# Transposes of the softmax blocks on the two row halves of the array

## The chip, the core and the metric

The kernel runs on one core of a Trainium2 chip. TensorE (PE) multiplies matrices and writes to PSUM, which has eight banks of 512 fp32 per partition; VectorE (DVE), ScalarE (ACT) and GpSimd (POOL) work on what lies in PSUM and SBUF, and DMA queues, issued by SyncE (SP), move data to and from HBM. The metric is the device time of one execution in microseconds.

## What is computed

Block-causal attention over 8 batches, 8 heads, 576 positions of 64 numbers, and an MLP block behind it with a layer norm:

```
scores = q @ k.T / 8, only where block_i >= block_j (blocks of 64 positions)
attn = softmax(scores);  x = attn @ v            # heads side by side: 512 columns
xn = (x - mean(x)) / sqrt(var(x) + 1e-6) * g
out = x + relu(xn @ w_ch1) @ w_ch2               # 512 -> 2048 -> 512
```

All inputs and the output are fp32.

## The kernel before

The first part of the time is attention. It goes by pairs of heads: 32 pairs, four to a batch. In a pair, each head's 64 numbers of q and k lie on one half of the 128 partitions, so the matmul of the scores uses 64 rows of the array, and the two heads use the two row halves (`mm`, L425; the planner's mode 64). The queries are taken 128 at a time: block rows i = 1 to 4, with 64 (2 i + 1) keys each. Rows 2 and 1 are the low scores (`s1`, two banks, softmax in the tile `pu`); rows 4 and 3 the high ones (`sab`, two tiles of two banks, softmax in `pab`). For each block row and head a pass on DVE (L443) copies the scores to SBUF, masks them and takes their extreme, which ends up in `nm`; ACT then makes the exponentials and their sums (L446).

For the products with v the keys must lie on the partitions, so each 128 x 128 cell of a softmax block is transposed on PE (`turn`, L455): `nc.tensor.transpose` with the cell as weights and the identity as moving operand, fp32. Four cells fill a PSUM bank (`new_tr`), which ACT or DVE copies to SBUF (`evac`, line 234 or 236 of the helper `copy`): two banks of the low blocks to `pt1`, four of the high blocks to `pt0`. Then come the products with v (`pv`, L461 and L465), each head on one column half of the array, first those that read `pt1`, then those that read `pt0`; DVE transposes the result to rows (L539), and a DMA writes them to HBM. Four of the eight banks hold the high scores, the other four are shared by low scores, transposes and products (one pool, `"tr"`). Once in eight pairs `first` does the first 64 queries of two batches; its own transposes (`across`) are no part of the change.

Beside that run the decoding of the weights (L350 to L373) and, once a batch is done, the normalisation of the first tiles of x (L678 to L774). The second part, after some 311 us, is the MLP: products with split weights (L876, L938), in which PE is busy nearly all the time.

The order on every engine is fixed when the program is built. `Plan` lists tasks with a guessed cost, a priority and the buffers that they read, write and allocate, runs them against a clock of its own, and emits them in that order; where a task may go to one of two engines (`any_of`), it takes the one that would be done first. On PE the steps of neighbouring pairs are chained by the numbers (pair, phase) given to `pe`: scores of pair k + 1 (phases 0 and 1), transposes of pair k (2 and 3), products of pair k (4.5 and 5). A task's `mode` only adds a guessed cost (`SWITCH`) when it differs from the one before on PE. At run time each engine goes through its list in order and waits on semaphores.

Of the kernel before, what the change touches and what calls it, by code (L numbers as in the profile page):

```python
# [18 lines left out]
P = 128  # L19
# [4 lines left out]
BIAS = {'PE': 0, 'SP': 0, 'DVE': 0, 'ACT': 0, 'POOL': 0}  # L24
WARM = 12
MMO = .0134
ROUNDS = 8, 8, 8, 8, 4
TILES = sum(ROUNDS)
D_0, D_1 = 12.0, .97
# [28 lines left out]
class Plan:  # L58
# [5 lines left out]
    def add(self, eng, cost=None, fn=None, r=(), w=(), prio=0.0, size=0, alloc=(), mode=128):  # L64
        k = Task(eng if isinstance(eng, dict) else {eng: (cost, fn)}, prio, size)
        k.mode = mode
        before = {}
        for x in r:
            before.update(dict.fromkeys(x.writers))
        for x in w:  # L70
            before.update(dict.fromkeys(x.readers))
        for x in r:
            x.readers.append(k)
        for x in w:
            x.writers.append(k)
        for x in before:
            x.next.append(k)
        k.left = len(before)
        k.uses = list(dict.fromkeys(x.root for x in (*r, *w, *alloc)))
        for x in k.uses:  # L80
            x.users += 1
        k.allocs = [x for x in dict.fromkeys(x.root for x in (*w, *alloc)) if x.make]
        self.tasks.append(k)
        return k
# [117 lines left out]
def attn_mlp_kernel(ctx: ExitStack, tc: tile.TileContext, qk, qk0, v, v0, w1, w2, g, out):  # L202
# [8 lines left out]
    nc = tc.nc  # L211
# [16 lines left out]
    def any_of(fn, **costs):  # L228

        return {e: (c, lambda e=e: fn(engines[e])) for e, c in costs.items()}  # L230
# [9 lines left out]
    def kind(name, shape, dtype, bufs, space=None, tag=None, most=None):  # L240

        tag = tag or name
        plan.free.setdefault(tag, bufs)
        own = (tag, "of " + name) if most else (tag,)
        if most:
            plan.free["of " + name] = most

        def make():
            return (space or sb).tile(shape, dtype, name=name, tag=tag, bufs=bufs)

        def new():
            x = Buf(own, make)
            if space is not dram and name not in ("tr", "s1", "o"):
                x.after, last[name] = [y for y in (last.get(name),) if y], x
            return x
        return new
# [17 lines left out]
    new_tr, new_s1, new_o, new_p = (kind(n, [P, 512], F32, 4, psum, "tr") for n in ("tr", "s1", "o", "p"))  # L274
# [7 lines left out]
    def small(name, shape, dtype, most):  # L282
        return kind(name, shape, dtype, 21, None, "small", most)
# [13 lines left out]
    new_t, new_tt, new_sum = small("t", [P, 512], F32, 4), small("tt", [P, 2, 2, P], F32, 4), small("sum", [P, 2, 256], F32, 2)  # L297
    xs = [kind(f"xm{p}", [P, max(ROUNDS) // 2, 2, 2, P], F32R, 1)() for p in range(7)]
    new_xw = kind("xw", [512, P], F32, 8, dram)
# [12 lines left out]
    ident = odd.tile([P, P], F32, name="ident")  # L312
# [72 lines left out]
    HALF = slice(0, 64), slice(64, 128)  # L385

    def evac(out, in_, n, **kw):
        add(any_of(lambda e: copy(e, out(), in_()), DVE=dve(n), ACT=act(n)), **kw)

    def pe(at, phase, *args, **kw):  # L390
        steps.setdefault((at, phase), []).append(add("PE", *args, **kw))
# [3 lines left out]
    def pair(k):  # L395
        b, c = k // 4, k % 4
        prio = 100 + 10 * k
        step = [0]

        def pr():  # L400
            step[0] += 1
            return prio + .05 * step[0]
# [24 lines left out]
        def cell(i, h, ck):  # L427

            at = FIRST[i] + (128 * i if ck == 0 else 128 * (i + ck) if h else 128 * (i - ck))
            return slice(at, at + P)  # L430
# [20 lines left out]
        def turn(o, slots):  # L451

            def go():
                for n, x in enumerate(slots()):
                    nc.tensor.transpose(o.t[:, n * P:(n + 1) * P], x, ident)  # L455
            return go

        def pv(o, at, z, steps):
            def go():
# [12 lines left out]
        pu = new_pu()  # L472
# [6 lines left out]
        low = [[], []]  # L479
# [5 lines left out]
        pab = big_of[k, 0] = new_pab()  # L485
# [8 lines left out]
        done = [[], []]  # L494
# [3 lines left out]
        pt0 = big_of[k, 1] = new_pt0()  # L498
        final[k] = [*done[0], *done[1]]
        got = []  # L500

        for h in range(2):
            for i in (4, 3):
                o, x = new_tr(), Buf(parent=pt0)
                if i == 4:
                    cells = [(4, h, ck) for ck in range(1, 5)]
                    need = [done[h][0]]
                else:
                    cells = [(3, h, ck) for ck in range(1, 4)] + [(3 + h, h, 0)]
                    need = [done[h][1]] + [done[x][1 - h] for x in range(2)]  # L510
                slots = lambda cells=cells: [pab.t[:, cell(*x)] for x in cells]
                pe(k + 1, 3, 4 * .112, turn(o, slots), r=list(dict.fromkeys(need)), w=[o], alloc=[pt0], prio=pr())
                evac(lambda h=h, i=i: pt0.t[:, h, :, i - 3], lambda o=o: o.t.rearrange("p (c n) -> p c n", c=4), 512,
                     r=[o], w=[x], prio=pr())
                got.append(x)
        ob, part_o = new_o(), []
        part_o.append(Buf(parent=ob))
        pe(k + 1, 5, (4 * 256 + 128) * 4 / 2400 + .06, pv(
# [2 lines left out]

        pt1 = new_pt1()
        got = []
        for h in range(2):
            o, x = new_tr(), Buf(parent=pt1)

            cells = (1, h, 1), (2, h, 1), (1 + h, h, 0), (2, h, 2)
            slots = lambda cells=cells: [pu.t[:, cell(*x)] for x in cells]
            need = low[h] + [low[x][1 - h] for x in range(2)]
            pe(k + 1, 2, 4 * .112, turn(o, slots), r=list(dict.fromkeys(need)), w=[o], alloc=[pt1], prio=pr())  # L530
            evac(lambda h=h: pt1.t[:, h].rearrange("p c i n -> p (c i n)"), lambda o=o: o.t, 512, r=[o], w=[x], prio=pr())
            got.append(x)
        part_o.append(Buf(parent=ob))
        pe(k + 1, 4.5, (2 * 256 + 128) * 4 / 2400 + .06, pv(
            ob, 0, lambda: pt1.t[:, :, 1, 0],
# [1 line left out]
            r=[v_sb, *got], w=[part_o[1]], alloc=[ot], prio=pr(), mode=1)  # L537

        add("DVE", dve(512), lambda: nc.vector.transpose(ot.t, ob.t), r=part_o, w=[ot], prio=pr())  # L539
        rows = Buf(parent=xd[b])  # L540
# [98 lines left out]
    n = 0  # L639
# [5 lines left out]
    END = 100 + 10 * NPAIR  # L645
    FROM = [sum(ROUNDS[:n]) for n in range(len(ROUNDS))]
    GROUPS = NJ // 2
# [3 lines left out]
    def norm_tiles(n, q, prio, gate):  # L651
# [4 lines left out]
        for h in range(2):  # L656
            t = FROM[n] + ROUNDS[n] // 2 * h + q
            m, r = divmod(t, 9)
# [95 lines left out]
    def operands(n, prio):  # L754

        tts = [new_tt() for _ in range(ROUNDS[n] // 2)]
        got = {}
# [22 lines left out]
        d1, d2, use1, use2 = {}, {}, {}, {}  # L780
        Q = range(ROUNDS[n] // 2)
        for q in Q:
# [76 lines left out]
    def products(n, gp, base):  # L859
# [8 lines left out]
        def product(p, x, start, r, w, at):  # L868
# [9 lines left out]
            new = Buf(parent=x)  # L878
            add("PE", 6 * (TN / 2400 + MMO), go, r=[*held[n, m], *wr, *r], w=[new, *w], prio=base + at)
            return new  # L880
# [42 lines left out]
    def second(n, gp, hs, base):  # L923
# [3 lines left out]
        for place, s in zip(PLACES[2 * half], (*range(half, 2 * half), *range(half))):  # L927
# [12 lines left out]
            for z, cut in enumerate(cuts):  # L940
                add("PE", 6 * ((cut.stop - cut.start) / 2400 + MMO), lambda go=go, cut=cut: go(cut),
                    r=[*final[NPAIR - 1], *hs[0, h][1], *hs[1, h][1], *wr], w=[parts[z]], alloc=[yb], prio=base + place + .1 * z)
# [85 lines left out]
```

## Time and profile before

| | |
|---|---|
| device time, median of 3 runs | 1050.25 us (1049.67 to 1051.68) |
| profiled execution, span from first to last instruction | 1051.5 us |
| PE busy | 1039.6 us (99%) |
| DVE busy | 743.6 us (71%) |
| ACT busy | 525.0 us (50%) |
| POOL busy | 285.8 us (27%) |
| transposes (L455) in the chain that ended last | 7% |
| granted TensorE clock, mean | 0.996 |

Shares are means over the two parts, which have different loads, so the first part is read by itself. The clock is given in parts of 2.4 GHz; 0.50 is 1.2 GHz. An instruction's time is from its start to its modelled end, and instructions overlap, so the pace of a run of them is the distance of their starts.

### The profile page before, as it was taken

How to read it: one execution, taken by the hardware profiler on the slowest of the kernel's cores; microseconds unless marked ns; L12 is line 12 of the kernel's file. 1: busy time of each engine (PE TensorE's matmuls, PEld its weight loads, DVE VectorE, ACT ScalarE, POOL GpSimd, SP SyncE). 2: the span in 40 equal slices, each digit the busy share in tenths (PEclk: the TensorE clock that was granted, in tenths of full speed). 3: DMA queues.
4: the chain of work that ended last, by engine and by line, in shares of the span. 5: the costliest groups of instructions: out<-in, count | busy, mean ns of one | idle time of the engine just before them, and what ended most of it. 6: DMA issues, size and time to landing. Idle time of an engine off the chain costs nothing.

```text
span 1051.5 us, 18007 instructions
## 1 busy us (share of the span) xinstructions
PE 1039.6 (99%) x6264; PEld 855.0 (81%) x6264; DVE 743.6 (71%) x1631; ACT 525.0 (50%) x1264; POOL 285.8 (27%) x468
## 2 busy tenths in 40 slices
PE   9999999999999999999999999999999999999998
PEld 7887777777778888888888888888888888888997
DVE  5878999789978878885656694665685565465544
ACT  7999897889984544441433341343242322122221
POOL 0223354445433755340222240222231220000000
PEclk9999999999999999999999999999999999999999
DMA  7678889898779898758787747688657667336873
GB/s 274 205 252 265 223 282 258 226 288 291 282 255 293 299 324 240 231 215 255 225 254 208 220 179 252 186 233 261 182 190 260 217 190 248 143 111 246 299 282 123
DMA packets 238682, 248.88 MB, mean 237 GB/s; under 512 B 159488, under 2 KB 189184, under 8 KB 228352
## 3 DMA queue, kind: packets, MB, share of 16 engines
q1 hardware_dynamic: 238592, 247.74, 73.1%
q8 instruction: 49, 0.80, 0.3%
q14 instruction: 41, 0.34, 0.1%
HBM read 182.68 MB, written 65.01 MB: 236 GB/s over the span
## 4 chain that ended last, share of the span: by engine, by line
PE 90%; DVE 6%; DMA 2%; ACT 1%; issue 1%; SPq 0%; POOL 0%; DVEq 0%; ACTq 0%; POOLq 0%
PE y L938 36%; PE p L876 32%; PE tr L455 7%; PE s L425 7%; PE o L465 5%; PE o L461 3%; DVE pab L443 1%; DMA x<-xd 1%; DMA was<-wa 1%; DVE pu L443 0%; DMA xrow<-x 0%; DVE ya L950 0%; DVE x L733 0%; DVE x L678 0%; DVE sgn L359 0%
## 5 line engine op out<-in xcount | busy, mean ns | idle before, releaser
L938 PE MATMUL y<-wc,h 128*128 128x512 f32 (+1 forms) x1740 | 434.0, 388 | 0.2 <-DVE h L896 0.2
L938 PEld LDWEIGHTS y<-wc,h 128*128 128x128 f32 x1740 | 323.0, 188 | 66.1 <-DVE h L896 1.3
L950 DVE TENSOR_TENSOR ya<-y,ya 128x512 f32<-128x512 f32 x290 | 198.0, 684 | 183.6 <-PE y L938 182.1
L876 PE MATMUL p<-xm,wa 128*128 128x512 f32 (+1 forms) x960 | 221.7, 368 | 0.0
L876 PEld LDWEIGHTS p<-xm,wa 128*128 128x128 f32 x960 | 169.9, 188 | 31.5 <-issue 0.2
L876 PE MATMUL p<-xm,wb 128*128 128x512 f32 (+1 forms) x720 | 166.3, 368 | 0.0
L884 ACT COPY t<-p 128x512 f32<-128x512 f32 (+1 forms) x120 | 65.3, 544 | 168.6 <-PE p L876 166.8
L876 PEld LDWEIGHTS p<-xm,wb 128*128 128x128 f32 x720 | 127.7, 188 | 23.6
L895 ACT ACTIVATE h<-t 128x512 fp32r<-128x512 f32 (+1 forms) x120 | 62.2, 579 | 163.5 <-DVE t L889 163.2
L889 DVE TENSOR_TENSOR t<-p,t 128x512 f32<-128x512 f32 (+1 forms) x120 | 76.3, 636 | 48.1 <-PE p L876 43.3
L425 PE MATMUL s<-raw 64*128 64x224 f32 (+3 forms) x768 | 97.6, 389 | 1.7 <-DVE nm L443 1.2
L234 ACT COPY pt<-tr 128x512 f32<-128x512 f32 x166 | 87.4, 597 | 9.1 <-PE tr L455 8.0
L446 ACT ACTIVATE pab<-pab,nm 128x448 f32<-128x448 f32 (+1 forms) x128 | 91.1, 730 | 0.1
L425 PEld LDWEIGHTS s<-raw 64*128 64x128 f32 x768 | 75.3, 189 | 17.8 <-issue 5.0
L443 DVE CUSTOM_DVE_ANT_0 pab<-s,never 128x448 f32<-128x448 f32 (+1 forms) x128 | 82.7, 684 | 2.5 <-PE s L425 1.9
L465 PE MATMUL o<-pt,v 128*64 128x256 f32 (+1 forms) x768 | 80.6, 345 | 0.0
L465 PEld LDWEIGHTS o<-pt,v 128*64 128x64 f32 x768 | 55.7, 138 | 28.3 <-issue 1.1
L896 DVE SCALAR_TENSOR_TENSOR h<-t,h 128x512 fp32r<-128x512 f32 (+1 forms) x120 | 74.1, 668 | 3.9 <-ACT h L895 3.8
L353 POOL TENSOR_SCALAR mag<-mag 128x512 f32<-128x512 f32 x32 | 48.7, 1523 | 100.0 <-ACT mag L350 92.1
L690 POOL TENSOR_SCALAR norm<-norm 128x1 f32<-128x1 f32 x28 | 7.2, 258 | 248.9 <-ACT xn L687 248.9
L446 ACT ACTIVATE pu<-pu,nm 128x320 f32<-128x320 f32 (+1 forms) x128 | 64.7, 509 | 19.9 <-DVE nm L443 18.9
L455 PE MATMUL tr<-ident,pab 128*128 128x128 f32 x512 | 65.0, 279 | 5.1 <-DVE nm L443 4.2
(96 smaller groups left out, 1035.6 us busy)
## 6 DMA issues: line engine op xcount, KB each, us to landing
wc<-wcs SPq DMA_DIRECT2D x40, 1024.0 KB, 7.1
wa<-was SPq DMA_DIRECT2D x32, 1024.0 KB, 6.4
wb<-wbs SPq DMA_DIRECT2D x32, 768.0 KB, 5.5
raw<-qk SPq DMA_DIRECT2D x31, 576.0 KB, 4.9
wr<-w SPq DMA_DIRECT2D x32, 512.0 KB, 6.2
v<-v SPq DMA_DIRECT2D x32, 320.0 KB, 5.2
x<-xd SPq DMA_DIRECT2D x144, 64.0 KB, 4.0
xrow<-x SPq DMA_DIRECT2D x36, 256.0 KB, 4.2
```

What stands on the lines that cost most here:

```text
L234: e.copy(out=out, in_=in_)
L425: nc.tensor.matmul(x, raw.t[HALF[h], 0, col], raw.t[HALF[h], 1, at:at + x.shape[1]], start=True, stop=True)
L443: add("DVE", dve(n) + .01, lambda: nc.vector.tensor_tensor_reduce(out=two(p.t[:, part(i, h)]), in0=mine(), in1=two(hide), scale=-0.125, sc ...
L446: add("ACT", act(n, True) + .14, lambda: nc.scalar.activation(out=p.t[:, part(i, h)], in_=p.t[:, part(i, h)], func=AF.Exp, bias=nm.t[:, at ...
L455: nc.tensor.transpose(o.t[:, n * P:(n + 1) * P], x, ident)
L465: nc.tensor.matmul(o.t[HALF[h], at + lo:at + 256], v_sb.t[:, ck, HALF[h]], rhs(h), start=False, stop=(n == len(steps) - 1), skip_group_che ...
L876: nc.tensor.matmul(x.t[:, 0:TN], w_(l), xs[m].t[:, 0:half, o, k], start=start and k == e == 0, stop=k == 1 and e == 2, skip_group_check=True)
L884: add("ACT", act(TN), lambda: nc.scalar.copy(out=t.t[:, 0:TN], in_=x.t[:, 0:TN]), r=[r], w=[new], prio=0)
L889: add("DVE", dve(TN), lambda: nc.vector.tensor_add(t.t[:, 0:TN], x.t[:, 0:TN], t.t[:, 0:TN]), r=r, w=[new], prio=0)
L896: add("DVE", dve(TN), lambda: nc.vector.scalar_tensor_tensor(out=x.t[:, 1, 0:TN], in0=src(), scalar=0.0, in1=x.t[:, 0, 0:TN], op0=ALU.max, ...
L938: nc.tensor.matmul(yb.t[:, cut], x.t[:, l, at:at + P], wc.t[:, i, o, cut], start=i == e == 0, stop=i == 1 and e == 2, skip_group_check=end)
L950: add("DVE", dve(cut.stop - cut.start), lambda yb=yb, ya=ya, cut=cut: nc.vector.tensor_add(ya.t[:, cut], yb.t[:, cut], ya.t[:, cut]), r=[p ...
```

## The change

A task now transposes eight cells. Each cell becomes two matmuls: the upper 64 queries on the upper half of the rows, the lower 64 on the lower half, each with 64 rows and 128 columns of weights and a 64 x 64 corner of the identity; they write 64 columns each to two different banks. A bank holds eight half cells, so there are as many banks to copy as before, six a pair, but two come with each task: one task of 16 matmuls for the low blocks and one for each head's high blocks. The copy puts its 512 numbers per partition into eight runs of 64 (`turned_to`). The tasks are given mode 64, that of the scores, and the guessed cost of a cell stays at 0.112 us (`TURN`).

```diff
+TURN = .112
...
                 for n, x in enumerate(slots()):
-                    nc.tensor.transpose(o.t[:, n * P:(n + 1) * P], x, ident)
+                    for rows, to in zip(HALF, o):
+                        nc.tensor.transpose(to.t[:, 64 * n:64 * n + 64], x[rows], ident[rows, rows])
             return go
+
+        def turned_to(pt, at, o, x, to):
+            for q, src in enumerate(o):
+                x.append(Buf(parent=pt))
+                evac(lambda q=q: to()[..., 64 * q:64 * q + 64],
+                     lambda src=src: src.t.rearrange("p (c i q) -> p c i q", c=4, q=64), 512, r=[src], w=[x[-1]], prio=at)
...
-            for i in (4, 3):
-                o, x = new_tr(), Buf(parent=pt0)
...
-                pe(k + 1, 3, 4 * .112, turn(o, slots), r=list(dict.fromkeys(need)), w=[o], alloc=[pt0], prio=pr())
-                evac(lambda h=h, i=i: pt0.t[:, h, :, i - 3], lambda o=o: o.t.rearrange("p (c n) -> p c n", c=4), 512,
-                     r=[o], w=[x], prio=pr())
-                got.append(x)
+            o = [new_tr(), new_tr()]
+            cells = [x for c in range(3) for x in ((3, h, c + 1), (4, h, c + 1))] + [(3 + h, h, 0), (4, h, 4)]
+            slots = lambda cells=cells: [pab.t[:, cell(*x)] for x in cells]
+            need = [*done[h], done[1 - h][1 - h]]
+            pe(k + 1, 3, 8 * TURN, turn(o, slots), r=list(dict.fromkeys(need)), w=o, alloc=[pt0], prio=pr(), mode=64)
+            turned_to(pt0, pr(), o, got, lambda h=h: pt0.t[:, h])
...
-        for h in range(2):
-            o, x = new_tr(), Buf(parent=pt1)
...
-            pe(k + 1, 2, 4 * .112, turn(o, slots), r=list(dict.fromkeys(need)), w=[o], alloc=[pt1], prio=pr())
-            evac(lambda h=h: pt1.t[:, h].rearrange("p c i n -> p (c i n)"), lambda o=o: o.t, 512, r=[o], w=[x], prio=pr())
-            got.append(x)
+        o = [new_tr(), new_tr()]
+        cells = [x for h in range(2) for x in ((1, h, 1), (2, h, 1), (1 + h, h, 0), (2, h, 2))]
+        slots = lambda: [pu.t[:, cell(*x)] for x in cells]
+        pe(k + 1, 2, 8 * TURN, turn(o, slots), r=[*low[0], *low[1]], w=o, alloc=[pt1], prio=pr(), mode=64)
+        turned_to(pt1, pr(), o, got, lambda: pt1.t.rearrange("p h c i n -> p (h c) i n"))
```

The change moves instructions, since the planner has other tasks to place. On PE, at the third pair's scores with the transposes and products of the second pair (`pt` of a lower number is `pt1`, the other `pt0`), before:

```order
L425 MATMUL s<-raw 128x224 x4
L455 MATMUL tr<-ident,pu 128x128 x8
L455 MATMUL tr<-ident,pab 128x128 x16
L461 MATMUL o<-pt_282,v 64x256 x2
L465 MATMUL o<-pt_282,v 64x256 x2
L465 MATMUL o<-pt_282,v 64x128 x2
L461 MATMUL o<-pt_300,v 64x256 x2
```

and now:

```order
L426 MATMUL s<-raw 128x224 x4
L457 MATMUL tr<-ident,pu 128x64 x16
L457 MATMUL tr<-ident,pab 128x64 x32
L469 MATMUL o<-pt_307,v 64x256 x2
L473 MATMUL o<-pt_307,v 64x256 x2
L473 MATMUL o<-pt_307,v 64x128 x2
L469 MATMUL o<-pt_332,v 64x256 x2
```

The steps stand in the same order; each transpose has become two. This holds for all pairs but the last two, where products of the MLP (L876, now L873) now stand between the steps.

On DVE, from the first pass over the high scores to the transpose of the output, in the third pair before (in the second it is `PP00PP`, with P a pass over `pab` and 0 or 1 a copy to `pt0` or `pt1`):

```order
L443 ISA pab_290,nm_274<-s_263,never_79 128x576
...
L443 ISA pab_290,nm_274<-s_263,never_79 128x448
...
L443 ISA pab_290,nm_274<-s_264,never_79 128x576
...
L236 COPY pt0_300<-tr_313 128x4x128
L443 ISA pab_290,nm_274<-s_264,never_79 128x448
...
L539 STREAM_TRANSPOSE ot_327<-o_326 128x512
```

Now the second pair (called pair 1 below, the first being pair 0) has two copies between the passes:

```order
L444 ISA pab_200,nm_161<-s_163,never_79 128x576
...
L237 COPY pt1_181<-tr_179 128x8x64
L444 ISA pab_200,nm_161<-s_163,never_79 128x448
...
L444 ISA pab_200,nm_161<-s_164,never_79 128x576
...
L237 COPY pt0_208<-tr_230 128x8x64
L444 ISA pab_200,nm_161<-s_164,never_79 128x448
...
L536 STREAM_TRANSPOSE ot_252<-o_251 128x512
```

and the third (pair 2) has its second copy behind all four:

```order
L444 ISA pab_327,nm_298<-s_287,never_79 128x576
...
L444 ISA pab_327,nm_298<-s_287,never_79 128x448
...
L444 ISA pab_327,nm_298<-s_288,never_79 128x448
...
L237 COPY pt0_332<-tr_331 128x8x64
L444 ISA pab_327,nm_298<-s_288,never_79 128x576
...
L237 COPY pt0_332<-tr_356 128x8x64
L536 STREAM_TRANSPOSE ot_376<-o_375 128x512
```

In each of them one copy has moved from ACT to DVE. Over the whole program DVE has 61 copies out of transpose banks instead of 30, ACT 135 instead of 166.

## Rows read from the trace of the kernel before

**Rows 1.** The page: busy time of each engine; the chain that ended last.

```profile
PE 1039.6 (99%) x6264; PEld 855.0 (81%) x6264; DVE 743.6 (71%) x1631; ACT 525.0 (50%) x1264; POOL 285.8 (27%) x468
...
PE y L938 36%; PE p L876 32%; PE tr L455 7%; PE s L425 7%; PE o L465 5%; PE o L461 3%; DVE pab L443 1%; DMA x<-xd 1%; DMA was<-wa 1%; DVE pu L443 0%; DMA xrow<-x 0%; DVE ya L950 0%; DVE x L733 0%; DVE x L678 0%; DVE sgn L359 0%
```

**Rows 2.** By stretch: length, busy us of each engine, clock, DMA share, GB/s.

```profile
19.25:311.00 291.75, 286.04 (x2737) 225.79 (x2736) 250.84 (x747) 261.69 (x704) 112.13 (x140) 0.99 0.81 255
311.00:1051.50 740.50, 736.84 (x3414) 616.01 (x3413) 482.39 (x849) 250.38 (x525) 172.97 (x323) 1.00 0.70 228
```

**Rows 3.** PE in order of time, one pair: start, length, what, count.

```profile
19.25 2.86 PE L425 MATMUL s<-raw 64*128 64x320 f32 x24
22.04 1.09 PE L455 MATMUL tr<-ident,pu 128*128 128x128 f32 x8
22.97 1.91 PE L455 MATMUL tr<-ident,pab 128*128 128x128 f32 x16
24.81 0.65 PE L461 MATMUL o<-pt,v 128*64 128x256 f32 x4
...
25.94 0.60 PE L461 MATMUL o<-pt,v 128*64 128x256 f32 x4
26.37 1.68 PE L465 MATMUL o<-pt,v 128*64 128x256 f32 x16
27.98 0.54 PE L425 MATMUL s<-raw 64*128 64x320 f32 x2
```

**Rows 4.** Weight loads (PEld) in order of time: a run's first, its first two.

```profile
22.04 0.14 PEld L455 LDWEIGHTS tr<-ident,pu 128*128 128x128 f32 x1 [0.28 <-issue]
...
22.04 0.20 PEld L455 LDWEIGHTS tr<-ident,pu 128*128 128x128 f32 x2 [0.28 <-issue]
```

**Rows 5.** PE in order of time: matmuls of 64 columns on four quarters.

```profile
36.72 0.69 PE L577 MATMUL tr<-qk 64*64 64x64 f32 x32
```

**Rows 6.** DVE in order of time, the same pair; in brackets idle time before.

```profile
22.14 0.76 DVE L443 CUSTOM_DVE_ANT_0 pab<-s,never 128x576 f32<-128x576 f32 x1 [0.26 <-PE s L425]
...
23.36 0.75 DVE L443 CUSTOM_DVE_ANT_0 pab<-s,never 128x576 f32<-128x576 f32 x1
...
24.48 0.69 DVE L236 COPY pt<-tr 128x512 f32<-128x512 f32 x1 [0.35 <-PE tr L455]
25.08 0.62 DVE L443 CUSTOM_DVE_ANT_0 pab<-s,never 128x448 f32<-128x448 f32 x1
...
28.10 0.72 DVE L539 STREAM_TRANSPOSE ot<-o 128x512 f32<-128x512 f32 x1 [2.39 <-PE o L465]
```

**Rows 7.** ACT in order of time, the same pair.

```profile
22.73 2.05 ACT L234 COPY pt<-tr 128x512 f32<-128x512 f32 x4
```

**Rows 8.** Groups by line: count, busy us, mean ns, idle us before.

```profile
L455 PE MATMUL tr<-ident,pab 128*128 128x128 f32 x512 | 65.0, 279 | 5.1 <-DVE nm L443 4.2
...
L234 ACT COPY pt<-tr 128x512 f32<-128x512 f32 x166 | 87.4, 597 | 9.1 <-PE tr L455 8.0 <-issue 0.2
...
L236 DVE COPY pt<-tr 128x512 f32<-128x512 f32 x30 | 20.7, 689 | 9.1 <-PE tr L455 8.6 <-PE tr L606 0.2
```

**Rows 9.** What DVE waited for, 0 to 315 us: total, times, longest.

```profile
DVE ot L539 <- PE o L465: 24.3, 22, 2.7
DVE pt L236 <- PE tr L455: 8.6, 21, 0.8
```

**Rows 10.** By stretch, as rows 2: the densest of DVE.

```profile
131.00:158.00 27.00, 27.00 (x247) 21.51 (x245) 25.48 (x80) 24.98 (x69) 14.80 (x26) 1.00 0.85 279
```

**Rows 11.** PE's two longest waits in a transpose stage; the stretches behind them.

```profile
179.26 0.63 PE L455 MATMUL tr<-ident,pab 128*128 128x128 f32 x4 [1.72 <-DVE nm L443]
...
193.79 2.45 PE L455 MATMUL tr<-ident,pab 128*128 128x128 f32 x12 [1.64 <-DVE nm L443]
...
180.50:184.00 3.50, 3.50 (x18) 2.57 (x18) 3.43 (x14) 2.96 (x8) 2.21 (x12) 0.51 1.04 381
194.00:197.70 3.70, 3.70 (x20) 2.80 (x20) 3.47 (x13) 2.60 (x7) 0.70 (x1) 0.54 0.96 173
```

More of the change, by code (lines that the diff above doesn't have):

```diff
@@ L502, in pair @@
         for h in range(2):
-            for i in (4, 3):
-                o, x = new_tr(), Buf(parent=pt0)
[L505 to L511, printed above, removed]
-                pe(k + 1, 3, 4 * .112, turn(o, slots), r=list(dict.fromkeys(need)), w=[o], alloc=[pt0], prio=pr())
-                evac(lambda h=h, i=i: pt0.t[:, h, :, i - 3], lambda o=o: o.t.rearrange("p (c n) -> p c n", c=4), 512,
-                     r=[o], w=[x], prio=pr())
-                got.append(x)
+            o = [new_tr(), new_tr()]
[4 more added lines that the diff above has]
+            turned_to(pt0, pr(), o, got, lambda h=h: pt0.t[:, h])
         ob, part_o = new_o(), []
@@ L523, in pair @@
         got = []
-        for h in range(2):
-            o, x = new_tr(), Buf(parent=pt1)
-            cells = (1, h, 1), (2, h, 1), (1 + h, h, 0), (2, h, 2)
-            slots = lambda cells=cells: [pu.t[:, cell(*x)] for x in cells]
-            need = low[h] + [low[x][1 - h] for x in range(2)]
-            pe(k + 1, 2, 4 * .112, turn(o, slots), r=list(dict.fromkeys(need)), w=[o], alloc=[pt1], prio=pr())
-            evac(lambda h=h: pt1.t[:, h].rearrange("p c i n -> p (c i n)"), lambda o=o: o.t, 512, r=[o], w=[x], prio=pr())
-            got.append(x)
+        o = [new_tr(), new_tr()]
[3 more added lines that the diff above has]
+        turned_to(pt1, pr(), o, got, lambda: pt1.t.rearrange("p h c i n -> p (h c) i n"))
         part_o.append(Buf(parent=ob))
```

## The prediction

> **What bounds the kernel now.** I read the page's totals first, then the table by stretch, then one pair on each engine in order of time, and last who waits for whom. TensorE is busy for 99% of the span, and the transposes are 7% of the chain that ended last [rows 1]. The change touches only the attention, so the stretch to look at is 19.25 to 311 us, 31 of the 32 pairs: there PE is busy 286.0 of 291.75 us, but VectorE (DVE) 250.8 and ScalarE (ACT) 261.7 [rows 2]. So PE sets the pace, and two engines stand close behind it. After 311 us PE is busy 736.8 of 740.5 us [rows 2], with nothing in it that the change makes shorter.
>
> One pair on PE [rows 3], counted from the start of its scores at 19.25: transposes of the pair before begin at 2.79, the products with v of its low blocks (pt1) at 5.56, those of its high blocks (pt0) at 6.69, the next scores at 8.73. Nothing lies between them but short turns of the mode: PE is the loop. DVE meanwhile makes four passes over the high scores (pab), one copy out of a transpose bank, and then stands 2.39 us until the products end [rows 6].
>
> **What PE saves.** Sixteen transposes take 1.91 us, of which the last is 0.28 long [rows 3, 8]: (1.91 - 0.28) / 15 = 109 ns each. A block becomes two matmuls of 64 columns on the two row halves. The halves of the scores already run side by side, but no row shows a transpose there, so its pitch is bounded: from below by half of 109, 54 ns; from above by the 32 matmuls of 64 columns on four quarters, 0.69 us for eight rounds, 86 ns [rows 5]. Between them lies the weight load: the first load of the transposes begins at 22.04 and takes 0.14, two of them 0.20, so the second begins 0.06 behind the first [rows 4]. I take 60 ns, since each half must load 128 columns per block and this row is the load itself. The saving is 24 x (109 - 60) = 1.18 us a pair (0.55 to 1.3).
>
> The turn from scores to transposes goes too, since both now use two row halves: the loads stood 0.28 us there [rows 4], some of which is the last scores running out, so 0.15 (0 to 0.28). The turn before the products with v stays. PE alone would need 8.73 - 1.33 = 7.40 us a pair, and 32 x 1.33 = 43 us less in all.
>
> The Trainium skill ("TensorE: Matmul & The Clock Gate", Part 2, LDWEIGHTS) speaks against this: a load takes its columns divided by 1.2, whatever the number of rows. By it 128 columns take 107 ns, two halves side by side still 107, and the 24 blocks would save 0.05 us instead of 1.18. Two loads that begin 0.06 us apart [rows 4] do not bear that out for transposes, but they are the first two of a run only; the first rival below is what it would make.
>
> **What the copies cost.** Before, each bank was full after four transposes and was copied by itself; now two banks fill together after sixteen half blocks, and the planner hands one to each engine. Counted from the order of instructions, DVE's copies go from 30 to 61 and ACT's from 166 to 135; the 30 and the 166 stand in the trace [rows 8]. Back to back a copy costs DVE 25.08 - 24.48 = 0.60 us [rows 6], and ACT (2.05 - 0.60) / 3 = 0.48, the last of four being 0.60 long [rows 7, 8]. So DVE gets 31 x 0.60 = 18.6 us more, ACT 14.9 less. The other pattern of the copy (runs of 64) I cost at nothing: as many elements in each partition; if it cost 10%, DVE would have 3.7 us more. Some casts of the weight decoding change sides as well; they are left out. In the last two pairs seven products of the first group of the MLP stand between the steps of attention; they fill waits of PE, and cost a wait if their weights are late.
>
> **Where a pair ends now.** Take 0.25 for a hand-over, from the 0.26 that DVE stood before its first pass [rows 6]. The scores end at 2.64 instead of 2.79, DVE's first pass begins at 2.74. Two passes take 23.36 - 22.14 = 1.22, so four 2.44.
> - In 11 pairs DVE copies early, in the manner pass, copy, pass, pass, copy, pass (pair 1 in the excerpts). Three passes (three quarters of 2.44) and two copies end at 2.74 + 1.83 + 1.20 = 5.77, and the pt0 products can begin at 6.02. PE itself would be there at 5.36: scores 2.64, transposes 24 x 0.06 = 1.44, the turn before pt1 (5.56 - 2.79 - 24 x 0.109 = 0.15), pt1 6.69 - 5.56 = 1.13. The pair is 6.69 - 6.02 = 0.67 shorter, not 1.33.
> - In 10 pairs the last copy stands behind all four passes (pair 2): 2.74 + 2.44 + 1.20 + 0.25 = 6.63. That is 0.06 shorter; in effect nothing. What is late next is DVE.
> - In the other 10, DVE has normalisation or decoding between the passes and already paces the pair; PE's saving turns into waiting, and DVE's second copy costs as much as its shorter waits give: 0 (-0.5 to +0.5).
>
> Sum: 11 x 0.67 + 10 x 0.06 + 0 = 8.0 us. A second way to it: DVE's 250.8 + 18.6 = 269.4 us must fit into the stretch [rows 2]; the densest stretch of some length has DVE busy 25.48 of 27 us [rows 10], 94.4%; at that density 269.4 takes 285.4, 6.4 less than 291.75. I take 6.5, nearer to the second, since it counts all that DVE has to do. The profiled execution spans 1051.5 us, 1.25 over the median of the runs, so I subtract from the median: 1050.25 - 6.5 = 1044.
>
> **Rivals.**
> - *The halves don't run at twice the rate* (loads of 128 columns bind, or the halves follow each other). The block stays near 109 ns, PE saves the turn alone, at most 32 x 0.15 = 4.8 us, and loses some of it as two banks now come free together. 1046 to 1052, at its middle 1049. For it: no transpose on half the rows in the trace. Against it: the 0.06 us.
> - *DVE packs tighter.* Its waits are nearly all waits for PE: 24.3 us for the products before the output transpose, 8.6 for transposes [rows 9]. If a faster PE takes most of them away, at 98% density the stretch takes 275 us: 1050 - 17 = 1033. Against it: DVE runs in order, and the second copy stands behind the passes.
> - *Slower: DVE keeps its waits.* Place: DVE's queue between the passes of one pair and the output transpose, where each copy now stands in order with decoding and normalisation. Price: the 18.6 us. It decides as soon as DVE's density stays under 269.4 / 291.75 = 92.3%; now it is 86%. At 91% the stretch takes 296.0: 1050 + 4 = 1054; at the present 86%, 313, 1071. For it: the passes can only begin when the scores end, and the scores only when the products end, so a wait in the loop comes back in each pair. Against it: the loops above are shorter or equal.
> - *The clock falls more often.* Twice in the attention PE waited 1.7 us in a transpose stage for DVE (1.72 <- DVE nm), and then the granted clock was 0.51 and 0.54 for 3.5 us, half of 2.4 GHz, before it was 1.0 again [rows 11]. Each such place costs some 1.7 us of PE's work. PE will now wait more, in just that stage; four more would take back the gain: 1050.
>
> **How the numbers follow.** About 0.2% (2.1 us) is what a measurement of this kernel can tell from no change. Forecast, a gain of 2 to 12 us: 0.46 (0.42 faster, 0.04 too near to 1048 to tell). Rate not doubled: 0.15 (0.05 faster, 0.08 same, 0.02 slower). Tighter packing: 0.13, faster. DVE keeps its waits: 0.18 (0.15 slower, 0.03 same). Clock: 0.08 (0.05 same, 0.03 slower). Together faster 0.60, same 0.20, slower 0.20. The range for 8 in 10 goes from half of the tighter packing to the 91% of the slower case: 1035 to 1055; the forecast's own is 1038 to 1048.
>
> **What would show it.** Right: sixteen half blocks in about 0.5 us on PE; scores and transposes without a wait of the loads between them; some 61 copies on DVE; DVE's waits for the products much shorter than 24 us; PE with new waits in front of the pt0 products, ended by copies; the attention over 5 to 8 us earlier and all behind it as long as before. Wrong: half blocks at 109 ns a block (first rival); DVE busy over 97% of the stretch (second); DVE's idle time in it still above 22 us with the end later (third); more than two stretches at half clock (fourth). A pair of the first kind that is not shorter than 8.4 us would refute the loop I worked out, whatever the total.

## The result and the profile after

The changed kernel takes 1059.71 us (median of 4 runs, 1059.30 to 1060.95), the kernel before 1050.97 (4 runs). The ratio is 1.009, with a 95% interval of 1.0074 to 1.0106: slower by 9 us, where 6 us faster was predicted, and above the range of 1035 to 1055. The profiled execution spans 1057.5 us.

The page of the kernel after: the busy line, and the chain that ended last, by engine and by line (compare [rows 1]).

```profile
PE 1019.6 (96%) x7032; PEld 835.2 (79%) x7032; DVE 752.7 (71%) x1636; ACT 515.0 (49%) x1251; POOL 292.1 (28%) x476
...
PE 74%; DVE 12%; ACT 5%; DMA 4%; issue 3%; POOL 2%; SPq 1%; DVEq 0%; POOLq 0%; ACTq 0%
PE y L935 35%; PE p L873 31%; PE o L473 4%; ACT pu L447 2%; DVE pab L444 2%; PE o L469 2%; PE s L426 2%; ACT pt L235 1%; DMA wcs<-wd 1%; DVE pt L237 1%; DVE pu L444 1%; DMA raw<-qk 1%; DVE sgn L360 1%; DVE xm L771 1%; PE tr L457 1%
```

TensorE lost 20 us of work and gained 26 us of standing (against a second profile of the kernel before, e0 below, it is 17 and 26). In the chain the transposes fell from 7% to 1%; in their place stand DVE's passes, ACT's low exponentials (`pu`, L447) and the copies (`pt`, L235 and L237). The attention, by stretch as in [rows 2]:

```profile
19.25:311.00 291.75, 261.00 (x3403) 203.85 (x3400) 254.27 (x750) 249.43 (x684) 112.67 (x143) 0.98 0.80 251
```

PE is busy 261.0 us instead of 286.0, DVE 254.3 (250.8) and ACT 249.4 (261.7), and the clock is 0.98. Nobody bounds this stretch; the engines wait for each other. One pair on PE in order of time, as in [rows 3]:

```profile
27.36 2.86 PE L426 MATMUL s<-raw 64*128 64x320 f32 x24
30.05 0.66 PE L457 MATMUL tr<-ident,pu 64*128 64x64 f32 x16
30.55 0.67 PE L457 MATMUL tr<-ident,pab 64*128 64x64 f32 x16
31.76 0.88 PE L457 MATMUL tr<-ident,pab 64*128 64x64 f32 x16 [0.55 <-ACT pt L235]
32.57 0.65 PE L469 MATMUL o<-pt,v 128*64 128x256 f32 x4
```

Eight blocks take 30.55 - 30.05 = 0.50 us, 62 ns each, and the transposes begin 2.69 us after the scores instead of 2.79. So the array does what the prediction said. But after two tasks, 1.2 us of work, all four banks of the pool are full, and the third task stands 0.55 us for a copy by ACT. Summed over the attention, groups as in [rows 8] (first two PE, then ACT and DVE):

```profile
L457 PE MATMUL tr<-ident,pab 64*128 64x64 f32 x1024 | 53.2, 230 | 24.3 <-ACT pt L235 18.7 <-DVE nm L444 2.9 <-DVE pt L237 2.4
L469 PE MATMUL o<-pt,v 128*64 128x256 f32 x256 | 43.1, 414 | 6.5 <-ACT pt L235 4.0 <-DVE pt L237 2.2
...
L235 ACT COPY pt<-tr 128x512 f32<-128x512 f32 x135 | 71.2, 581 | 2.6 <-PE tr L457 1.2 <-issue 1.1 <-ACT pu L447 0.2
...
L237 DVE COPY pt<-tr 128x512 f32<-128x512 f32 x61 | 41.5, 682 | 0.2
```

The high transposes wait 24.3 us instead of 5.1, the first products 6.5; 18.7 + 4.0 = 22.7 us of that is for ACT's copies, 4.6 for DVE's. What DVE and ACT in turn wait for, 19.25 to 311 us (total, times, longest; compare [rows 9]; the last line is ACT's in the kernel before):

```profile
DVE ot L536 <- PE o L473: 28.1, 17, 4.1
ACT pu L447 <- DVE nm L444: 23.9, 27, 2.7
...
ACT pu L446 <- DVE nm L443: 14.2, 12, 2.2
```

That closes a loop: products, output transpose on DVE, low passes on DVE, low exponentials on ACT, copies on ACT, transposes, products. Pair 10, one of those that the prediction took for 0.67 us shorter, shows it. Its scores start at 91.82, the next pair's at 101.01: 9.2 us, not 8.1.

```profile
91.82 2.86 PE L426 MATMUL s<-raw 64*128 64x320 f32 x24
91.94 0.72 DVE L536 STREAM_TRANSPOSE ot<-o 128x512 f32<-128x512 f32 x1 [0.24 <-PE o L473]
...
92.99 0.49 DVE L444 CUSTOM_DVE_ANT_0 pu<-s,never 128x320 f32<-128x320 f32 x1 [0.33 <-PE s L426]
...
93.58 0.56 ACT L447 ACTIVATE pu<-pu,nm 128x320 f32<-128x320 f32 x1 [0.20 <-DVE nm L444]
...
94.37 1.29 DVE L360 SCALAR_TENSOR_TENSOR sgn<-wr,sgn 128x512 int32<-128x512 int32 x1
...
95.13 0.44 ACT L447 ACTIVATE pu<-pu,nm 128x192 f32<-128x192 f32 x1
...
95.57 1.52 ACT L235 COPY pt<-tr 128x512 f32<-128x512 f32 x3
95.59 0.74 DVE L444 CUSTOM_DVE_ANT_0 pab<-s,never 128x576 f32<-128x576 f32 x1
...
96.19 0.27 PE L457 MATMUL tr<-ident,pab 64*128 64x64 f32 x1 [0.50 <-ACT pt L235]
96.27 0.07 DVE L444 DVE_READ_ACCUMULATOR2_ANT nm<- 128x1 f32 x1
96.27 0.68 DVE L237 COPY pt<-tr 128x512 f32<-128x512 f32 x1
...
96.67 0.71 PE L457 MATMUL tr<-ident,pab 64*128 64x64 f32 x15 [0.21 <-ACT pt L235]
...
98.08 0.68 DVE L237 COPY pt<-tr 128x512 f32<-128x512 f32 x1
...
98.91 0.65 PE L469 MATMUL o<-pt,v 128*64 128x256 f32 x4 [0.30 <-DVE pt L237]
```

ACT's first copy starts at 95.57, 3.75 us after the scores, behind four low exponentials (the first at 93.58) that stand behind the low passes and the output transpose. A task needs two free banks, and they come one after the other: the first half block goes at 96.19, the other fifteen matmuls at 96.67. On DVE a decode step of 1.29 us (L360) stands ahead of the first high pass, which so begins 3.77 us after the scores. The step is not new there. In the kernel before (e0, below), where this pair's scores start at 91.05, DVE has it at the same place, but it takes 0.69 us, the pass begins 3.16 us after the scores, and the pair takes 8.74 us:

```profile
93.60 0.69 DVE L359 SCALAR_TENSOR_TENSOR sgn<-wr,sgn 128x512 int32<-128x512 int32 x1
94.21 0.62 DVE L443 CUSTOM_DVE_ANT_0 pab<-s,never 128x448 f32<-128x448 f32 x1
```

Why the step is longer in the changed kernel is not shown.

In two places the clock falls too. PE and ACT at 210 to 222 us, and stretches there as in [rows 11]:

```profile
210.56 0.71 PE L457 MATMUL tr<-ident,pab 64*128 64x64 f32 x15
214.88 1.12 PE L457 MATMUL tr<-ident,pab 64*128 64x64 f32 x16 [3.60 <-ACT pt L235]
215.93 1.12 PE L469 MATMUL o<-pt,v 128*64 128x256 f32 x4
...
212.82 0.66 ACT L351 ACTIVATE mag<-wr 128x512 f32<-128x512 f32 x1 [3.07 <-issue]
...
214.26 1.54 ACT L235 COPY pt<-tr 128x512 f32<-128x512 f32 x3
```

```profile
210.00:214.00 4.00, 1.27 (x30) 1.07 (x27) 3.50 (x12) 1.18 (x4) 2.48 (x12) 1.00 1.01 379
214.00:221.00 7.00, 6.12 (x42) 4.02 (x44) 3.64 (x6) 6.77 (x18) 4.15 (x3) 0.51 0.85 284
221.00:225.00 4.00, 4.00 (x56) 3.32 (x54) 3.10 (x11) 1.59 (x8) 0.00 (x0) 1.00 0.44 119
```

ACT stood 3.07 us in front of a step of the weight decoding (L351), with two low exponentials and the copies queued behind; PE waited 3.6 us, and the next 6.8 us went at 0.51, half of 2.4 GHz. The profile names no releaser, but the words that L351 reads were still on their way. Their transfer and, for all 16 of its line, the times to landing:

```profile
202.61 0.42 SPq L346 DMA_DIRECT2D wr<-w  x1
...
DMA to landing us min/median/max: 3.5/6.0/10.1
```

This one is the longest, 10.1 us, so it landed at 212.7, and L351 begins at 212.82. A stretch of 3.4 us at half clock at 265 us, behind waits of 0.51, 0.21 and 0.65 us, is the only other one in the attention.

These two places hold most of the loss. The pairs in which they lie, from scores to scores, in the kernel after and then in e0:

```profile
206.84:221.57 14.73, 11.12 (x110) 8.29 (x105) 10.19 (x29) 9.03 (x24) 8.66 (x18) 0.77 0.91 330
258.97:270.66 11.69, 10.33 (x139) 7.65 (x137) 9.96 (x27) 8.99 (x24) 7.63 (x8) 0.85 0.75 268
...
206.64:216.16 9.52, 9.52 (x87) 7.44 (x81) 9.38 (x31) 7.01 (x21) 7.60 (x19) 1.00 0.99 307
253.53:262.89 9.36, 9.36 (x114) 7.46 (x112) 8.79 (x26) 9.04 (x26) 7.13 (x7) 1.00 0.90 338
```

They are 5.2 and 2.3 us longer, 7.5 of the 8.0 us by which this part grows (table below). Over all other pairs gains and losses come to 0.5 us: what the transposes save there, waits take back.

For the rest I use one sum, made from all of PE's rows: the time from the first scores to the 73rd matmul of the MLP's first group (L873; L876 before), split into time without any matmul (idle) and the rest (occupied). A wait counts as idle only from the modelled end of the last matmul, some 0.2 us behind the pace, so the occupied time holds a little of each wait. The first row is a second profile of the kernel before (experiment e0, below).

| kernel | total us | occupied | idle |
|---|---|---|---|
| before, again (e0) | 326.8 | 319.7 | 7.1 |
| after | 334.8 | 302.6 | 32.2 |
| after's order, old transposes (e1) | 332.0 | 323.3 | 8.7 |
| after, ordered for its true pace (e12) | 320.4 | 298.8 | 21.6 |
| e12's order, old transposes (e14) | 330.1 | 323.2 | 6.8 |

After loses 8.0 us in this part, 25.1 of new idle against 17.1 of work saved. Another 1.2 us is lost by the second round of the MLP (its 401st matmul of L873 comes 9.2 us later than in e0), and nothing behind it.

### The profile page after: what moved, and what is told of

It reads as the page before. It is cut to its first block, busy times and chain, and to the rows that moved or that the text cites. A ratio compares the mean times of both kernels' runs of the same rounds, so it can differ in the third digit from the quotient of the medians.

```text
span 1057.5 us, 19502 instructions
## 1 busy us (share of the span) xinstructions
PE 1019.6 (96%) x7032; PEld 835.2 (79%) x7032; DVE 752.7 (71%) x1636; ACT 515.0 (49%) x1251; POOL 292.1 (28%) x476
## 4 chain that ended last, share of the span: by engine, by line
PE 74%; DVE 12%; ACT 5%; DMA 4%; issue 3%; POOL 2%; SPq 1%; DVEq 0%; POOLq 0%; ACTq 0%
PE y L935 35%; PE p L873 31%; PE o L473 4%; ACT pu L447 2%; DVE pab L444 2%; PE o L469 2%; PE s L426 2%; ACT pt L235 1%; DMA wcs<-wd 1%; DVE pt L237 1%; DVE pu L444 1%; DMA raw<-qk 1%; DVE sgn L360 1%; DVE xm L771 1%; PE tr L457 1%
## 5 line engine op out<-in xcount | busy, mean ns | idle before, releaser
L873 PE MATMUL p<-xm,wa 128*128 128x512 f32 (+1 forms) x960 | 222.3, 368 | 0.5 <-ACT pt L235 0.5
L873 PEld LDWEIGHTS p<-xm,wa 128*128 128x128 f32 x960 | 169.7, 188 | 32.3 <-ACT pt L235 0.8
L873 PE MATMUL p<-xm,wb 128*128 128x512 f32 (+1 forms) x720 | 166.8, 368 | 0.0
L873 PEld LDWEIGHTS p<-xm,wb 128*128 128x128 f32 x720 | 127.5, 188 | 23.8 <-issue 0.2
L447 ACT ACTIVATE pab<-pab,nm 128x576 f32<-128x576 f32 (+1 forms) x128 | 91.5, 723 | 1.1 <-DVE nm L444 0.9
L426 PEld LDWEIGHTS s<-raw 64*128 64x128 f32 x768 | 74.9, 188 | 16.2 <-issue 5.0
L444 DVE CUSTOM_DVE_ANT_0 pab<-s,never 128x576 f32<-128x576 f32 (+1 forms) x128 | 83.4, 682 | 3.0 <-PE s L426 2.3
L473 PE MATMUL o<-pt,v 128*64 128x256 f32 (+1 forms) x768 | 83.2, 352 | 0.0
L473 PEld LDWEIGHTS o<-pt,v 128*64 128x64 f32 x768 | 60.3, 141 | 26.2 <-issue 3.2
L447 ACT ACTIVATE pu<-pu,nm 128x192 f32<-128x192 f32 (+1 forms) x128 | 63.8, 500 | 30.1 <-DVE nm L444 28.6
L457 PE MATMUL tr<-ident,pab 64*128 64x64 f32 x1024 | 53.2, 230 | 24.3 <-ACT pt L235 18.7
L235 ACT COPY pt<-tr 128x512 f32<-128x512 f32 x135 | 71.2, 581 | 2.6 <-PE tr L457 1.2
```

The costliest lines, as they stand in the source:

```text
L235: e.copy(out=out, in_=in_)
L426: nc.tensor.matmul(x, raw.t[HALF[h], 0, col], raw.t[HALF[h], 1, at:at + x.shape[1]], start=True, stop=True)
L444: add("DVE", dve(n) + .01, lambda: nc.vector.tensor_tensor_reduce(out=two(p.t[:, part(i, h)]), in0=mine(), in1=two(hide), scale=-0.125, sc ...
L447: add("ACT", act(n, True) + .14, lambda: nc.scalar.activation(out=p.t[:, part(i, h)], in_=p.t[:, part(i, h)], func=AF.Exp, bias=nm.t[:, at ...
L457: nc.tensor.transpose(to.t[:, 64 * n:64 * n + 64], x[rows], ident[rows, rows])
L473: nc.tensor.matmul(o.t[HALF[h], at + lo:at + 256], v_sb.t[:, ck, HALF[h]], rhs(h), start=False, stop=(n == len(steps) - 1), skip_group_che ...
```

## The experiments

Times are medians; the ratio is to the kernel before on the same chip, with its 95% interval.

**Is the first profile of before typical?** e0 is the kernel before, unchanged.

> The kernel before once more, for a second profile: its first spans 1051.5 us, 1.25 over the median, with two stretches at half clock, while all changed kernels so far span 2 to 3 us less than their medians. If the first profile was one of the slower executions: a span of 1046 to 1049 and no or fewer stretches at half clock. If not: 1050 to 1052 with the two stretches in the same places.

1050.31 us, ratio 0.9996 (0.9981 to 1.0011), span 1048.4, and in the attention:

```profile
19.25:311.00 291.75, 285.91 (x2749) 225.77 (x2746) 253.10 (x750) 261.16 (x704) 114.00 (x142) 1.00 0.82 259
```

The clock is 1.00 throughout. The profile in [rows 11] had two stretches at half clock that this one lacks, and spans 3.1 us more. So spans of other kernels are set against 1048.4, and the two clock falls that the prediction started from are not in every execution.

**Order or rate?** e1 keeps the order and the tasks of after, with the old transposes of 128 queries:

```
-                    for rows, to in zip(HALF, o):
-                        nc.tensor.transpose(to.t[:, 64 * n:64 * n + 64], x[rows], ident[rows, rows])
+                    nc.tensor.transpose(o[n // 4].t[:, P * (n % 4):P * (n % 4) + P], x, ident)
```

> The changed kernel's order on every engine, but each transpose is one matmul of 128 queries again (109 ns a block), four to a bank, in the turn of the mode of before. Bank theory (PE fills the four free banks and then waits until ACT and DVE, in their fixed order, have copied): the rate buys waits, so this is within 4 us of the changed kernel, 1056 to 1064. The prediction's theory (the rate is worth 6 to 13 us in this order): 1066 to 1072. DVE-load theory (31 more copies on DVE pace the pairs): as the changed kernel, 1058 to 1062.

1056.97 us, 1.0066 (1.0049 to 1.0083). Some 6.5 us of the loss are there without any half transpose: the new tasks and the order that comes with them cost that. The table says how the rest comes: from e1 to after PE has 20.7 us less to do and stands 23.5 us longer. In this order the faster array is worth less than nothing. By pairs, though, the one with the late transfer is 4.7 us longer than in e1 (10.03) and the other with half clock 1.1 (10.59); all the rest together is 3.0 us shorter.

**Is it DVE's load?** The prediction's slower rival priced the 31 copies that move to DVE. e2 binds five of six copies to ACT (25 on DVE, 171 on ACT, close to before):

```
+                if mixed and q:
                     evac(...)
+                else:
+                    add("ACT", act(512), lambda q=q, src=src: copy(nc.scalar, ...), r=[src], w=[x[-1]], prio=at)
```

> The changed kernel with five of a pair's six copies bound to ACT and the sixth free, so that DVE has 25 copies and ACT 171, about as before the change (30 and 166). DVE-load theory: the 36 copies of 0.60 us that DVE loses come back, 1040 to 1048. Bank theory: both banks of a task now wait for ACT one after the other, so PE waits as long or longer, 1056 to 1066.

1063.18 us, 1.0124 (1.0109 to 1.0139): slower still. e9 does the same with the old transposes:

> Transposes of 128 queries as before (109 ns a block), but in tasks of eight blocks with two banks each, and five of six copies on ACT as in e2_copies_act: 25 copies on DVE, 171 on ACT. Against the kernel before only the grouping by two banks and the order that follows from it are new. Order theory: 1054 to 1063, near to e2_copies_act. DVE-load theory: as the kernel before, 1048 to 1052.

1060.94 us, 1.0092 (1.0067 to 1.0118). With pace and copies as before, tasks of two banks cost 10 us. So the copies that moved to DVE are not the cause. Both runs have an order of their own and more copies on ACT, for which PE waits; they say nothing of the rest of DVE's list, which e4 tries.

**Is it what stands ahead of the copies?** e4 cuts the two decode passes on DVE (L360, L363) from 512 to 32 columns, in the same order; e5 does that in the kernel before.

```
-            out=sgn(), in0=wv(1), scalar=-2147483648, in1=sgn(), ...
+            out=sgn()[:, 0:32], in0=wv(1)[:, 0:32], scalar=-2147483648, in1=sgn()[:, 0:32], ...
```

> The changed kernel in its own order, with DVE's two passes of the weight decoding cut from 512 columns to 32, so that some 25 x 2 x 0.5 = 25 us of DVE's work are gone from the attention (the weights are not decoded). DVE-load theory: 1037 to 1046. Bank theory: DVE's waits grow instead, 1053 to 1060.

> Control for e4_short_decode: the kernel before, in its own order, with the same two decoding passes on DVE cut from 512 columns to 32 (the weights are not decoded). If what the cut gives in the changed kernel (8.5 us) is DVE's load there, the kernel before, which PE paces, gives at most a few us: 1046 to 1051. If decoding costs both alike: 1040 to 1044.

e4: 1051.22 us, 1.0013 (1.0003 to 1.0022), 8 us less than after. e5: 1047.81, 0.9974 (0.9963 to 0.9985), 3 us less than before. e4 lies between the ranges of the two theories that were named for it, and bears out neither. The same cut is worth three times as much in the changed kernel: DVE's list now lies in PE's way. Of the idle, though, 27.9 of 32.2 us stay (the same sum for e4); it is a part of the cause.

e6 and e7 take 768 columns a pair away from ACT's exponentials, once from the low ones, which stand ahead of the copies, once from the high ones, which stand behind:

```
+            cut = lambda x: x[:, 0:64] if i < 3 else x       # e6; e7: x[:, 0:320] if i > 2 else x
-                out=p.t[:, part(i, h)], in_=p.t[:, part(i, h)], func=AF.Exp, ...
+                out=cut(p.t[:, part(i, h)]), in_=cut(p.t[:, part(i, h)]), func=AF.Exp, ...
```

> The changed kernel in its own order, with ACT's exponentials over the low blocks, which stand ahead of the copies in ACT's list, cut to 64 columns each: 768 columns a pair fewer, some 0.64 us of ACT's work (the rest of the low blocks stays without exponential). Order theory (PE's faster transposes stand until ACT, behind these exponentials, copies two banks): 1047 to 1055. DVE-load theory: ACT is not what paces, 1056 to 1060.

> As e6_short_low_exp, with the same 768 columns a pair cut from the exponentials over the high blocks instead (to 320 columns each), which stand mostly behind the copies in ACT's list. Order theory: ACT's load is the same as in e6, but the copies come no earlier, 1056 to 1060. If ACT's total load counts instead of its order, this is as fast as e6.

e6: 1055.67 us, 1.0056 (1.0039 to 1.0074); e7: 1058.87, 1.0086 (1.0065 to 1.0108). By the ratios, as many columns less give 3.6 us ahead of the copies, and 0.4 behind them, which is nothing that the intervals can tell. It is the place, not ACT's total; but e6 stays 0.7 us above the range that the order theory gave it, so these exponentials are a small part. In the profiles, 4.4 of e4's 7.5 us and 3.8 of e6's 4.1 (the sum of the table) lie in the two pairs that hold most of the loss (above); e7 gains 1.9 us there and loses 1.4 in others.

**One half of the change alone.** e10 halves the transposes of the low blocks only, e11 those of the high blocks only; the others as before.

> The change on the low blocks alone (8 of a pair's 24), the high ones transposed as before in four banks by themselves. Order theory: the high blocks' banks come free one by one again, and PE stands less: 1049 to 1054. If each halved transpose cost the same: a third of the change's 9 us, 1053.

> The change on the high blocks alone (16 of 24), the low ones as before. Order theory: both tasks of the high blocks need two banks at once, behind banks that wait for copies: 1055 to 1061, nearly all of the change's cost. If each halved transpose cost the same: 1056.

e10: 1051.85 us, 1.0016 (1.0001 to 1.0031); e11: 1071.32, 1.0192 (1.0165 to 1.0219). The parts don't add up: 1.7 and 20.2 us against 9 for both, and e11 lies 10 us above what either theory gave it. Each edit gives the planner another puzzle, and the order that comes out matters more than the edit.

**Ordered for the true pace.** `TURN` = 0.112 tells the planner the old pace. e3 and e8 change that number alone, to 0.062 and 0.08 (72 and 71 copies on DVE).

> The changed kernel with the planner's guess for a block at 0.062 us, the pace that its trace shows, instead of 0.112; only the order changes, and copies move ahead of exponentials and passes (72 copies on DVE, 124 on ACT). Bank theory: copies come earlier, banks come free earlier, 1042 to 1053. DVE-load theory: DVE has 11 copies more than in the changed kernel, 6.6 us more work, 1060 to 1068.

> The changed kernel with the planner's guess for a block at 0.08 us; only the order changes. e3 (0.062) had its attention 8 us ahead of the kernel before and lost more than that behind it, where the operands of the MLP's second round came late. Order theory: the attention again ahead of the kernel before, and if the second round is not late, 1043 to 1050. DVE-load theory: 1058 to 1064.

e3: 1063.11 us, 1.0122 (1.0107 to 1.0137); e8: 1053.92, 1.0038 (1.0024 to 1.0052). The total of e3 falls in the range of the DVE-load theory, but not for its reason, and e8 lies between its two ranges, with its attention level with e0's (330.9). e3's attention is the fast one that was looked for: its 73rd matmul of L873 starts at 325.9 us, e0's at 330.9, after's at 338.9. It is lost later, at 430 to 505 us: PE's group there, and ACT's wait for a transfer (total, times, longest).

```profile
L873 PE MATMUL p<-xm,wa 128*128 128x512 f32 x71 | 20.0, 430 | 12.0 <-DVE xm L771 9.6 <-ACT t L881 1.4 <-DVE xm L237 1.0
```

```profile
ACT xm L235 <- DMA xt<-xw: 20.8, 2, 12.7
```

The normalised tiles of the second round come late. e12 therefore sets `TURN` to 0.062 and gives that normalisation an earlier due time; e13 is the kernel before with the earlier due time alone, e14 is e12 with the old transposes (as in e1).

```
-TURN = .112
+TURN = .062
...
-... if n == 0 else END + 2 * n - 10,
+... if n == 0 else END + 2 * n - 14,
```

> The changed kernel with two numbers of the planner changed: the guessed cost of a cell at 0.062 us, which is the measured pace, instead of 0.112, and the normalisation of the MLP's later rounds seven eighths of a group of products earlier (END + 2 n - 14 instead of - 10). The first number alone (run e3) had the attention 5 to 8 us ahead of the kernel before, and then lost some 18 us to TensorE waiting at 440 to 500 us for tiles whose transfer and normalisation came late. Theory 'the halving pays, the order took it': the attention is ahead as in e3 and the late tiles are in time, so 1040 to 1046. Rival 'the order of the attention decides and any new order costs': attention as in the changed kernel, 1052 to 1062. Rival 'the second round is short of transfer, not of order': attention ahead, but the wait at 440 to 500 us remains over 8 us, 1052 to 1062.

> Control: the kernel before with the earlier normalisation alone. If that edit gives something by itself, what e12 gains is not the transposes'. Both theories: 1048 to 1052, since in the kernel before TensorE does not wait for these tiles; over 3 us from 1050.5 on either side would change how e12 is read.

> The same two numbers as in e12, with transposes of 128 queries at 109 ns, four to a bank, in place of the halves at 62 ns; tasks of two banks, modes and copies as in e12. If TensorE's pace is worth something in this order, it is slower than e12 by up to 24 x 0.047 us a pair, 36 us in all, and I expect 10 to 25. If waits for copies hide the pace, as between e1 and the changed kernel, it lies within 4 us of e12.

| run | us | ratio to before | 95% interval |
|---|---|---|---|
| e12 | 1045.79 | 0.9958 | 0.9942 to 0.9974 |
| e13 | 1049.53 | 0.9997 | 0.9986 to 1.0009 |
| e14 | 1055.55 | 1.0051 | 1.0035 to 1.0067 |

e12 beats both kernels: 4.3 us faster than before, 13.9 than after. The due time gives the kernel before nothing (e13), and the old transposes in e12's order are 9.8 us slower (e14), just under the 10 to 25 that were expected. So the halving does pay, once the order is made for it. In the table, from e14 to e12 PE has 24.4 us less to do and gives 14.8 back as idle; in after's order it gave back 23.5 against 20.7. The attention of e12 by stretch, its high transposes and first products, DVE's copies, and PE's first products of weights at 430 to 505 us:

```profile
19.25:311.00 291.75, 271.34 (x3513) 212.40 (x3510) 266.05 (x766) 252.88 (x687) 114.44 (x144) 0.99 0.82 256
...
L457 PE MATMUL tr<-ident,pab 64*128 64x64 f32 x1024 | 52.2, 230 | 17.3 <-ACT pt L235 12.6 <-DVE nm L444 2.7 <-DVE pt L237 1.3
L469 PE MATMUL o<-pt,v 128*64 128x256 f32 x256 | 42.7, 412 | 1.6 <-ACT pt L235 1.0 <-DVE pt L237 0.4
...
L237 DVE COPY pt<-tr 128x512 f32<-128x512 f32 x72 | 47.9, 682 | 2.1 <-PE tr L457 1.7
...
L873 PE MATMUL p<-xm,wa 128*128 128x512 f32 x90 | 22.4, 389 | 0.0
```

DVE has eleven copies more than in after, and PE waits less: 17.3 and 1.6 us instead of 24.3 and 6.5. That is a third sign against the copies on DVE as the cause. The wait for the second round is gone.

## Why the prediction was wrong

**Right: the array.** The block takes 62 ns (60 predicted, 54 to 86 as bounds), the turn from scores to transposes shrank by 0.10 us (0.15). The first rival, halves not at twice the rate, falls. The rule that the prediction weighed (the Trainium skill, "TensorE: Matmul & The Clock Gate", Part 2, LDWEIGHTS: columns divided by 1.2, by estimate 107 ns for a block) is not borne out for these transposes: 62 ns, in which each row half takes a load of 128 columns.

**Right: the copies.** 61 on DVE; they cost 41.5 - 20.7 = 20.8 us more (18.6 predicted), at 682 ns each against 689 in [rows 8], so the runs of 64 cost nothing. ACT has 16.2 us less (14.9).

**Wrong: the term "11 pairs x 0.67" and the loop behind it.** This is the step that failed, and the runs show where.
- It gave 0.67 us each to 11 pairs. Behind pair 2, six pairs show their four passes and two copies in just that order in the trace (those whose scores start at 27.36, 56.35, 91.82, 139.96, 157.28 and 290.52). They take 54.3 us together, against 54.1 in e0, where 6 x 0.67 = 4.0 less was predicted; only the one at 139.96, with 8.32, is under 8.4.
- It timed DVE's queue from a first high pass 2.74 us after the scores' start. In pair 10 that pass begins at 3.77, since a decode step of 1.29 us stands ahead of it; even in e0, with the step at 0.69 us, it begins at 3.16. From there on it went as worked out: three passes and two copies end 98.76 - 95.59 = 3.17 us later, 3.03 predicted, and the products begin 7.09 after the scores instead of 6.02. The pair takes 9.2 us, above the 8.4 that the prediction named as its refutation.
- It had no term for ACT's copies, of which there are fewer. But 22.7 us of PE's waits are for ACT's copies and 4.6 for DVE's. Before, the copies had to keep up with four transposes in 0.44 us, one bank at a time. Now PE fills all four banks in 1.2 us and then needs two at once, and ACT's copies stand behind low exponentials that hang, through DVE, on the end of the last products. e6 (3.6 us) and e4 against e5 (5 us more than in before) show both lists to matter. The largest single wait, 3.6 us, came with a transfer that landed late, which the prediction had no term for either.

The second way to the sum, DVE at 94.4% density, failed with it: DVE is busy 254.3 of 291.75 us, 87%. It took the density of a stretch in which PE was the bound for one that holds without that.

**The order as a term of its own was missing.** The prediction argued from single steps in an order that it saw to be nearly the same on PE. e1 shows 6.5 us lost with the pace as before, as much as the whole gain that was forecast.

**The rivals.** "DVE keeps its waits" had the right sign, the right sign to look for (DVE idle over 22 us in the stretch, here 37.5) and the right place, the loop from products to scores. Its price, 31 copies on DVE, was wrong: fewer copies there, and more on ACT, made it worse (e2, e9), and more went with the best kernel (e12). "The clock falls more often" took part: 6.8 and 3.4 us at half clock against none in e0, which costs at most half of these 10.2 us, 5.1. That is two stretches, not the more than two that it was to be known by. But e1, at a clock of 1.00 in the attention, shows most of the loss without it. The 0.20 for slower was too little for a loop in which PE was so closely followed, with ACT and DVE 30 and 41 us from filling the stretch [rows 2].

**Open.** Why tasks of two banks cost 6.5 to 10 us at the old pace (e1, e9) is not taken apart into the grouping, the mode given to the planner and the places of the copies. In the table it is 3.6 us of occupied time and 1.6 of idle for e1, and the former has no mechanism shown. Nor is it settled why e11 alone costs 20 us. No run moves the late transfer in front of L351 alone, so its share of the loss is read from the trace and not tested. And orders of the changed kernel lie up to 17 us apart (e12, e3), while the kernel before was planned afresh only for the due time (e13): another order might give it 4 us as well. That the halving pays is shown at e12's order (e12 against e14), not against the best order of the old tasks.

## What to carry to other kernels

When the bounding engine gets faster on one step, time the whole loop through the engines that hand it its buffers, in their own order of instructions, and count the buffers that it will now want at once. Where the order is planned from guessed costs, a changed step needs its true cost in the plan, and what was just in time later in the program has to be looked at again: with both, the same change went from 9 us slower to 4 us faster. Look also at the sum pair by pair: most of a loss can lie in one or two of them. An order that looks the same on the bounding engine may differ by 7 us; the way to see it is the new order with the old step.

## What the runs showed of the hardware

- Two fp32 transposes of 64 queries on the two row halves run side by side: 62 ns for both, where one of 128 queries takes 109 ns.
- A PSUM copy in eight runs of 64 costs DVE the same as one in four runs of 128: 682 against 689 ns.
- After PE had waited 3.6 us between transposes the granted clock was 0.51 for 6.8 us, at 214 us of the kernel after; at 265 us it was at half for 3.4 us behind waits of at most 0.65 us. In e1, with the same order, old transposes and waits of at most 1.06 us, it was 1.00 over the whole attention.
